# Sparse attention and MoE in one kernel: query chunks shifted by one block, units dealt to steps by time

## The chip, the core and the metric

One core of a Trainium2 chip runs one launch. The time is the device time of that launch in microseconds; what is compared is the median of several runs. TensorE (PE) does matmuls and transposes, VectorE (DVE) and ScalarE (ACT) the elementwise work, GpSimd (POOL) copies and issues transfers, SyncE (SP) only issues transfers. Sixteen DMA engines carry what all of them issue.

## The reference

Block-sparse attention over four batches, eight heads, 768 positions in 24 blocks of 32, head size 64. Each query block sees its neighbours, the first and the last block, and three sampled blocks; the first and the last query block see everything. The result, as 3072 tokens of width 512, goes through a two-layer network.

```python
scores = scale * np.matmul(q, k.transpose(0, 1, 3, 2))
mask = np.abs(blk_i - blk_j) <= window                      # window = 1
mask = mask | (blk_i == 0) | (blk_j == 0) | (blk_i == n_blocks - 1) | (blk_j == n_blocks - 1)
for qb in range(n_blocks):
    for kb in sampled_blocks[qb]:
        mask[qb * block:(qb + 1) * block, kb * block:(kb + 1) * block] = True
scores = np.where(mask, scores, -1000000000.0)
...
out = np.matmul(attn, v)                                    # attn: softmax of scores
...
h = x @ w_in                                                # 512 to 2048
g = h * (1.0 / (1.0 + np.exp(-beta * h)))
return g @ w_out                                            # 2048 to 512
```

## The kernel before

**Chunks and steps.** A batch's 24 query blocks form six chunks of four blocks (128 tokens). A *step* treats one chunk and one half Q of the heads (four heads), so there are 12 steps in a batch and 48 in all. Two chunks of each batch hold a global query block: chunk 0 holds block 0 as its first, chunk 5 holds block 23 as its last. `CHUNK_ORDER` (L48) is 1, 2, 0, 5, 3, 4.

**Keys and values of a chunk.** For each ordinary query block a row of 256 keys is put together in `KG` (`gather_chunk`, L239): 96 neighbours by one copy for the chunk (L248), the first and the last block (L253, only when one of the three buffers is first used in a batch), and three sampled blocks (L259, one copy of 32 columns each, from a register that holds the block's number). Values are gathered from a table in DRAM, `vtab` (`gather_v`, L263): `VA` holds the neighbours and block 0 (L281, L284), `VB` the sampled blocks and the last one. For the blocks of a chunk that are in `direct`, `VB` is fetched by SP, three transfers of 32 rows for each block (L297); for the others by one indirect transfer from GpSimd (L278). Three `VA` and three `VB` buffers go round, and so do three `KG` buffers.

**A step.** `scores` (L303) puts 16 small matmuls into two PSUM banks; VectorE takes the negated maximum (`nm`, L327), ScalarE the exponentials (`probs`, L330). One step later `probs_T` (L337) transposes them on PE, and VectorE copies the result (L345). Another step later `attend` (L384) multiplies by the values: 32 small matmuls for four ordinary blocks (L392), and for a chunk with a global block 24 of these and 24 more over all keys (L404). VectorE divides by the row sum (L410, L411). After both halves of a chunk, `x_transpose` (L427) turns the chunk's output for the network.

**Global query blocks.** `global_scores` (L348) computes both global blocks of two head pairs against all 768 keys: a *global pass*, four in a batch, each with two maxima on VectorE (L364) and two exponentials on ScalarE (L369). `global_T` (L375) transposes it. The layout within a pass is block 0, block 23 for one pair, then for the next. In batch 0 two passes run in step 3 and one each in steps 4 and 5; in later batches one in each of steps 2 to 5 of the batch.

**The network.** Chunks are grouped as `sizes` (L416) says: 2, 2, then five groups of 4. When a group's last chunk is turned, `push_group` (L478) appends 16 first-layer units (`h_unit`, L442: four matmuls, a tanh on ScalarE, a product on VectorE) and the second-layer units of the group before (of the first two groups its own) (`o_unit`, L460: eight matmuls; two units make a chunk's tile, which ScalarE scales and stores, L471 and L473) to one queue, `moe_q`. Each step takes an equal number of units: those in the queue, divided by the steps until the next group is complete (L649 to L654). They are spread over the step around its other work by shares (L721 to L735).

**Order.** The order on PE, GpSimd and SP is that of the program text; each engine works its queue off in order, and a wait holds up all that stands behind it. On GpSimd's queue stand the key gathers, indirect transfers, casts of the next batch (L200, L223) and all loads after the first six: w_in in four pieces (L172), w_out in four (L176), k, q and v of the next batches (L86).

**The opening.** Step 0 starts with half of the heads of two chunks gathered by GpSimd (`kg_half(0, 0)`, `kg_half(1, 0)`, L594 and L595). The other half comes from VectorE in steps 1 and 2 (L667, L674). For the first two chunks one block of four is fetched by SP and three by GpSimd (L600, L601). w_in is issued in step 1 and 2, w_out in steps 5 to 7.

Of the kernel before, what the change touches and what calls it, by code (L numbers as in the profile page):

```python
# [20 lines left out]
def kernel(  # L21
# [26 lines left out]
    CHUNK_ORDER = [1, 2, 0, 5, 3, 4]  # L48
# [106 lines left out]
    def load_regs(t, engine, top, c):  # L155
        i0, i1 = max(4 * c, 1), min(4 * c + 4, NB - 1)
# [82 lines left out]
    def gather_chunk(b, c, KG, p0, p1, eng=None, steady=False):  # L239
        eng = eng or nc.gpsimd  # L240
        js = [j for j in range(4) if 0 < 4 * c + j < NB - 1]
# [3 lines left out]
        for w0 in range(p0, p1, 2):  # L245
            base = kv[:, w0:w0 + 2, (4 * c + j0 - 1) * BLK:(4 * c + j0 + 2) * BLK]
# [10 lines left out]
        for j in js:  # L257
            for r in range(3):
                eng.tensor_copy(  # L259
                    out=KG[:, j, p0:p1, 128 + BLK * r:160 + BLK * r],  # L260
                    in_=kv[:, p0:p1, bass.ds(k_regs[(4 * c + j, r)] * BLK, BLK)])

    def gather_v(b, c, direct=()):  # L263
# [3 lines left out]
        js = [j for j in range(4) if 0 < 4 * c + j < NB - 1]  # L267
# [8 lines left out]
        for j in js:  # L276
            if j not in direct:
                nc.gpsimd.indirect_dma_start(  # L278
                    VB[:, j, :], None, tab[:, :],
                    bass.IndirectOffsetOnAxis(idx_b[:, 4 * c + j:4 * c + j + 1], 0))  # L280
        nc.sync.dma_start(out=VA[0:96, js[0]:js[0] + nj, :],  # L281
                          in_=rows((4 * c + js[0] - 1) * BLK, 96, BLK, nj))
        ga = [j for j in js if 4 * c + j != 1]
        nc.sync.dma_start(out=VA[96:128, ga[0]:ga[0] + len(ga), :],  # L284
                          in_=rows(0, BLK, 0, len(ga)))
        if len(ga) != nj:
            nc.sync.dma_start(out=VA[96:128, 1, :], in_=tab[S:S + BLK, :])
        if direct:
            v_regs = load_regs(sb_eff, ET.SP, NB, c)
            gb = [j for j in direct if 4 * c + j != NB - 2]  # L290
            nc.sync.dma_start(out=VB[96:128, gb[0]:gb[0] + len(gb), :],
                              in_=rows(S - BLK, BLK, 0, len(gb)))
            if len(gb) != len(direct):
                nc.sync.dma_start(out=VB[96:128, NB - 2 - 4 * c, :], in_=tab[S:S + BLK, :])
            for j in direct:
                for r in range(3):
                    nc.sync.dma_start(  # L297
                        out=VB[BLK * r:BLK * (r + 1), j, :],
                        in_=tab[bass.ds(v_regs[(4 * c + j, r)] * BLK, BLK), :])
# [3 lines left out]
    def scores(b, c, Q, KG):  # L303
# [6 lines left out]
        for hp in range(2):  # L310
            for pr in range(2):
                pg = 2 * Q + pr
                for j in range(4):
                    i = 4 * c + j
                    rr = slice(64 * hp, 64 * hp + 64)
                    if 0 < i < NB - 1:
# [31 lines left out]
    def global_scores(b, Q, hp):  # L348
        rr = slice(64 * hp, 64 * hp + 64)
        halves = []  # L350
        for s in range(2):
            sct = ring.tile([P, 512], FP32, tag="bank", name="scg")[:, 0:384]
            halves.append(sct)
            for j in range(4):
                pr, blk = j // 2, (j % 2) * (NB - 1)
# [28 lines left out]
    def attend(b, c, Q, ptT, VA, VB, gTs, x16):  # L384
        av = ring.tile([P, 512], FP32, tag="bank", name="av")[:, 0:4 * VW].rearrange(
            "p (u e) -> p u e", e=VW)
        js = [j for j in range(4) if 0 < 4 * c + j < NB - 1]
# [9 lines left out]
        if len(js) < 4:  # L397
            j = 0 if c == 0 else 3
            bi = 0 if c == 0 else 1
            for u in range(4):  # L400
                pr, hp = u // 2, u % 2
                jj = 2 * pr + bi
                for ct in range(6):
                    nc.tensor.matmul(av[BLK * j:BLK * (j + 1), u, :],  # L404
                                     lhsT=gTs[hp][:, ct, BLK * jj:BLK * (jj + 1)],
                                     rhs=v16[b][:, ct, 4 * Q + u, :],
                                     start=(ct == 0), stop=(ct == 5),
                                     tile_position=(0, BLK * j))
# [51 lines left out]
    def o_unit(gi, s, part):  # L460
# [7 lines left out]
        if part == 1:  # L468
# [3 lines left out]
            r0 = b * S + c * P  # L472
            nc.scalar.dma_start(out=out[r0:r0 + P, :], in_=osb)  # L473
# [28 lines left out]


    steps = []
    for b in range(B):
        for (c, Q) in ((1, 0), (2, 0), (1, 1), (2, 1), (0, 0), (5, 0), (0, 1), (5, 1),
# [273 lines left out]
```

## Time and profile before

| | |
|---|---|
| median of 3 runs | 341.94 us (340.7 to 342.27) |
| the profiled execution | 341.41 us |
| its span, first to last instruction | 339.6 us |
| PE busy | 292.8 us (86%) in 4288 matmuls |
| VectorE busy | 222.4 us (65%) |
| ScalarE busy | 225.7 us (66%) |
| GpSimd busy | 174.3 us (51%) |
| moved by DMA | 56.95 MB |

A profile page gives each engine's busy time, then the span in 40 equal slices (each digit is the busy share of a slice in tenths), the chain of work that ended last, and groups of instructions by source line. Busy time by stretch gives the same for chosen stretches, with PE's granted clock, the mean busy share of the DMA engines (transfers overlap, so it can exceed 1) and GB/s. In a timeline a line has start, length, engine, source line, operation, what it writes from what, and how many are merged. Idle time of an engine that sets nothing costs nothing, and a busy PE need not be at its peak, since matmuls are pipelined.

### The profile page before, as it was taken

The numbers are of one execution on the slowest core, as the hardware profiler recorded it, in microseconds if no ns is written. First come the engines' busy times: TensorE is split into PE (matmuls) and PEld (weight loads), VectorE is DVE, ScalarE is ACT, GpSimd is POOL, SyncE is SP. The second block draws the span as 40 slices with busy tenths as digits, with TensorE's granted clock in tenths as the row PEclk, the third lists the DMA queues.
The fourth block names the chain that finished last, engine by engine and source line by source line (L and its number), as shares of the span: only waits on it lengthen the run. The fifth ranks groups of instructions, "written<-read, shape, count | busy, mean of one in ns | idle before, by whom it ended". The sixth has DMA issues, their size and how long they took to land.

```text
span 339.6 us, 11327 instructions
## 1 busy us (share of the span) xinstructions
PE 292.8 (86%) x4288; PEld 166.1 (49%) x4288; DVE 222.4 (65%) x506; ACT 225.7 (66%) x447; POOL 174.3 (51%) x451
## 2 busy tenths in 40 slices
PE   0554898669787999887999999999989999899995
PEld 0342556545555565544455565454555554444442
DVE  3666878624859777899686668677997576534400
ACT  1693579943768799887688987667776545335411
POOL 5659985629889955879696519725131200000000
PEclk9999999979969999999799999999999999999999
DMA  6979999997698992659898327724162510000021
GB/s 169 377 230 202 292 252 326 274 225 239 169 286 207 314 268 51 173 137 294 183 306 251 75 68 191 178 59 115 35 184 68 135 57 33 31 33 31 32 93 64
DMA packets 40135, 56.95 MB, mean 168 GB/s; under 512 B 7280, under 2 KB 31984, under 8 KB 40080
## 3 DMA queue, kind: packets, MB, share of 16 engines
q0 software_dynamic: 10160, 26.21, 29.2%
q1 hardware_dynamic: 24400, 23.71, 25.7%
q10 hardware_dynamic: 5520, 6.30, 5.4%
q8 instruction: 34, 0.56, 0.7%
q14 instruction: 21, 0.17, 0.2%
HBM read 50.77 MB, written 9.62 MB: 178 GB/s over the span
## 4 chain that ended last, share of the span: by engine, by line
PE 57%; DVE 14%; DMA 10%; ACT 10%; issue 3%; POOL 3%; SPq 1%; another core or an unknown queue 0%; POOLq 0%; DVEq 0%; ACTq 0%
PE ops L465 21%; PE hps L448 19%; PE tp_p L341 5%; ACT probs L330 5%; DVE nm L327 4%; DVE g L454 4%; DMA w_out_sb<-in_moe_w_out_dram 4%; DMA st_kq<-in_k_dram 4%; PE sc L320 3%; PE av L392 3%; DMA st_q<-in_q_dram 3%; ACT t_sb L452 2%; PE av L404 2%; DVE gnm L364 2%; PE tp_x L434 1%
## 5 line engine op out<-in xcount | busy, mean ns | idle before, releaser
L448 PE MATMUL hps<-xT,w_in_sb 128*128 128x512 f16 (+1 forms) x448 | 99.2, 360 | 1.9 <-DVE gnm L366 0.7
L454 DVE SCALAR_TENSOR_TENSOR g<-t_sb,hps 128x512 f16<-128x512 f16 (+1 forms) x112 | 66.8, 609 | 46.9 <-ACT t_sb L452 44.2
L465 PE MATMUL ops<-w_out_sb,g 128*128 128x512 f16 x384 | 89.6, 379 | 3.8 <-DMA w_out_sb<-in_moe_w_out_dram 3.8
L452 ACT ACTIVATE t_sb<-hps,beta_h_sb 128x512 f16<-128x512 f32 (+1 forms) x112 | 70.3, 647 | 29.4 <-PE hps L448 26.4
L330 ACT ACTIVATE probs<-sc,nm 128x256 f16<-128x256 f32 x192 | 76.9, 485 | 18.2 <-DVE nm L327 14.3
L327 DVE TENSOR_REDUCE nm<-sc 128x2 f32<-128x512 f32 x96 | 62.9, 684 | 20.0 <-PE sc L320 16.5
L278 POOL DMA_INDIRECT VB<-vtab,idx_b x40 | 38.9, 972 | 71.5 <-PE av L392 55.9
L259 POOL COPY KG<-kT 128x128 f16 (+1 forms) x264 | 62.8, 293 | 3.0 <-PE sc L320 1.9
L448 PEld LDWEIGHTS <-w_in_sb 128*128 128x128 f16 x448 | 42.8, 101 | 35.3 <-issue 5.2
L465 PEld LDWEIGHTS <-g 128*128 128x128 f16 x384 | 36.8, 98 | 45.8 <-issue 4.7
L248 ACT COPY KG<-kT 128x768 f16<-128x768 f16 (+1 forms) x44 | 34.6, 793 | 11.3 <-PE sc L320 7.1
L345 DVE COPY probsT<-tp_p 128x1024 f16<-128x1024 f16 x48 | 32.3, 673 | 4.8 <-PE hps L448 1.7
L341 PE MATMUL tp_p<-identity,probs 128*128 128x128 f16 x384 | 32.2, 231 | 1.2 <-ACT probs L330 0.6
L471 ACT ACTIVATE osb<-ops 128x512 f32<-128x512 f32 x24 | 14.4, 601 | 28.0 <-PE ops L465 27.9
L320 PE MATMUL sc<-KG,qT 64*32 64x256 f16 x704 | 25.0, 294 | 7.5 <-DVE KG L259 5.1
L341 PEld LDWEIGHTS <-probs 128*128 128x128 f16 x384 | 23.9, 103 | 5.2 <-issue 2.0
L392 PEld LDWEIGHTS <-probsT 128*32 128x32 f16 x1408 | 17.4, 100 | 18.1 <-issue 14.1
L369 ACT ACTIVATE gp<-scg,gnm 128x384 f16<-128x384 f32 x32 | 16.9, 581 | 13.7 <-DVE gnm L366 7.5
L392 PE MATMUL av<-VA,probsT 128*32 128x65 f16 x704 | 22.1, 203 | 2.8 <-issue 2.7
L392 PE MATMUL av<-VB,probsT 128*32 128x65 f16 x704 | 21.8, 201 | 2.9 <-DMA VB<-vtab 2.2
L411 DVE TENSOR_TENSOR x<-av,rec 128x256 f16<-128x256 f32 x48 | 20.1, 420 | 0.8
L207 PE MATMUL tp_k<-identity,k 128*128 128x128 f16 x96 | 9.1, 242 | 12.3 <-ACT k L200 12.1
(69 smaller groups left out, 280.1 us busy)
## 6 DMA issues: line engine op xcount, KB each, us to landing
VA<-vtab SPq DMA_DIRECT2D x16, 390.0 KB
out_dram<-osb ACTq DMA_DIRECT2D x24, 256.0 KB
VB<-vtab SPq DMA_DIRECT2D x147, 32.5 KB
st_k<-in_k_dram POOLq DMA_DIRECT2D x6, 768.0 KB
st_q<-in_q_dram POOLq DMA_DIRECT2D x6, 768.0 KB, 9.3
st_v<-in_v_dram POOLq DMA_DIRECT2D x6, 768.0 KB, 9.7
VA<-vtab SPq DMA_DIRECT2D x8, 292.5 KB
vtab<-v POOLq DMA_DIRECT2D x3, 780.0 KB
```

The costliest lines, as they stand in the source:

```text
L248: (nc.scalar.copy if steady else nc.vector.tensor_copy)(out=KG[:, j0:j1, w0:w0 + 2, 0:96], in_=dataclasses.replace(base, ap=[ap[0], [BLK, ...
L259: eng.tensor_copy(out=KG[:, j, p0:p1, 128 + BLK * r:160 + BLK * r], in_=kv[:, p0:p1, bass.ds(k_regs[(4 * c + j, r)] * BLK, BLK)])
L278: nc.gpsimd.indirect_dma_start(VB[:, j, :], None, tab[:, :], bass.IndirectOffsetOnAxis(idx_b[:, 4 * c + j:4 * c + j + 1], 0))
L320: nc.tensor.matmul(scs[hp][BLK * j:BLK * (j + 1), pr, :], lhsT=qT[b][rr, pg, i * BLK:(i + 1) * BLK], rhs=rhs, start=True, stop=True, tile_ ...
L327: nc.vector.tensor_reduce(out=nm[:, hp, :], in_=scs[hp], axis=AX.X, op=ALU.max, negate=True)
L330: last_exp[0] = nc.scalar.activation(out=pt[:, 2 * pr + hp, :], in_=scs[hp][:, pr, :], func=AF.Exp, bias=nm[:, hp, pr:pr + 1], scale=1.0)
L341: nc.tensor.transpose(out=tp[:, u * 256 + half * P:u * 256 + (half + 1) * P], in_=pt[:, u, half * P:(half + 1) * P], identity=identity)
L392: nc.tensor.matmul(av[BLK * j:BLK * (j + 1), u, :], lhsT=ptT[:, u, half, BLK * j:BLK * (j + 1)], rhs=V[:, j, h * VW:(h + 1) * VW], start=( ...
L448: nc.tensor.matmul(hp[:, 0:n], lhsT=w_in_sb[:, cc, f * P:(f + 1) * P], rhs=xT_tiles[gi][:, cc, 0:n], start=(cc == 0), stop=(cc == N_DMC - 1))
L452: nc.scalar.activation(out=t_sb[:, 0:n], in_=hp[:, 0:n], func=AF.Tanh, bias=0.0, scale=beta_h_sb[:, f:f + 1])
L454: nc.vector.scalar_tensor_tensor(out=g_tiles[gi][:, f, 0:n], in0=t_sb[:, 0:n], scalar=1.0, in1=hp[:, 0:n], op0=ALU.add, op1=ALU.mult)
L465: nc.tensor.matmul(op, lhsT=g_tiles[gi][:, f, s * P:(s + 1) * P], rhs=w_out_sb[:, f, :], start=(f == 0), stop=(f == N_FFC - 1))
```

## The change

**Chunks.** Chunk c now holds blocks 4c - 1 to 4c + 2, so chunk 0 holds blocks 23, 0, 1 and 2, and the others have four ordinary blocks. The order is 1, 2, 3, 4, 5, 0, in pairs of chunks. A chunk's rows in the output are contiguous except chunk 0's, which are stored in two transfers.

**Global rows.** The pass now lays out block 23 before block 0, so that both global rows of a pair stand side by side. `attend` computes them together for chunk 0: 24 matmuls with 64 columns of weights instead of twice 24 with 32. In batch 0 the passes run in steps 4, 5, 10 and 11, in later batches in steps 1 to 4 of the batch.

**The opening.** The second halves of the first two key gathers go from VectorE to GpSimd; the first w_in piece is issued before the values of the first two chunks, of which SP now fetches all four blocks. Of the third and fourth chunk SP fetches three blocks, in chunk 0 of batch 0 both, in chunk 0 of later batches one; elsewhere two. The transposes of batch 1's k and q move one step later.

**Dealing.** A unit has a cost in PE columns: 4096 for a second-layer unit, for a first-layer unit four times the tokens of its group (at least 320). A step's budget is the cost of all units in the queue, divided by one step more than there are until the next group; units are run until a target is met, and what a step overruns or leaves over is carried to the next.

```diff
-    CHUNK_ORDER = [1, 2, 0, 5, 3, 4]
+    CHUNK_ORDER = [1, 2, 3, 4, 5, 0]
...
-        js = [j for j in range(4) if 0 < 4 * c + j < NB - 1]
+        js = [2, 3] if c == 0 else [0, 1, 2, 3]
...
-                    i = 4 * c + j
+                    i = (4 * c + j - 1) % NB
...
-                pr, blk = j // 2, (j % 2) * (NB - 1)
+                pr, blk = j // 2, (NB - 1, 0)[j % 2]
...
-        if len(js) < 4:
-            j = 0 if c == 0 else 3
-            bi = 0 if c == 0 else 1
+        if c == 0:
             for u in range(4):
                 pr, hp = u // 2, u % 2
-                jj = 2 * pr + bi
                 for ct in range(6):
-                    nc.tensor.matmul(av[BLK * j:BLK * (j + 1), u, :],
-                                     lhsT=gTs[hp][:, ct, BLK * jj:BLK * (jj + 1)],
+                    nc.tensor.matmul(av[0:2 * BLK, u, :],
+                                     lhsT=gTs[hp][:, ct, 2 * BLK * pr:2 * BLK * (pr + 1)],
                                      rhs=v16[b][:, ct, 4 * Q + u, :],
                                      start=(ct == 0), stop=(ct == 5),
-                                     tile_position=(0, BLK * j))
+                                     tile_position=(0, 0))
...
-            nc.scalar.dma_start(out=out[r0:r0 + P, :], in_=osb)
+            if c > 0:
+                nc.scalar.dma_start(out=out[r0:r0 + P, :], in_=osb)
+            else:
+                nc.scalar.dma_start(out=out[b * S:b * S + 96, :], in_=osb[BLK:P, :])
+                nc.scalar.dma_start(out=out[(b + 1) * S - BLK:(b + 1) * S, :],
+                                    in_=osb[0:BLK, :])
...
+    def moe_cost(f, a):
+
+        return 8 * D_MODEL if f is o_unit else N_DMC * max(320, P * len(groups[a[0]]))
+
+    moe_done = [0.0]
+
+    def run_moe_to(target):
+
+        while moe_q:
+            cost = moe_cost(*moe_q[0])
+            if moe_done[0] + 0.5 * cost > target:
+                break
+            run_moe(1)
+            moe_done[0] += cost
...
-        for (c, Q) in ((1, 0), (2, 0), (1, 1), (2, 1), (0, 0), (5, 0), (0, 1), (5, 1),
-                       (3, 0), (3, 1), (4, 0), (4, 1)):
+        for (c, Q) in ((1, 0), (2, 0), (1, 1), (2, 1), (3, 0), (4, 0), (3, 1), (4, 1),
+                       (5, 0), (5, 1), (0, 0), (0, 1)):
...
-                trs[5 + a] += [tr("kkqq"[a], a % 2, 0), tr("kkqq"[a], a % 2, 1)]
+                trs[6 + a] += [tr("kkqq"[a], a % 2, 0), tr("kkqq"[a], a % 2, 1)]
...
-                direct = {0: (1, 2, 3), 5: (0, 1, 2)}
+                direct = {0: (2, 3), 3: (0, 1, 2), 4: (0, 1, 2)}
             else:
-                direct = {0: (1, 2), 5: (0, 1)}
+                direct = {0: (2,)}
...
-    prefetch_v(0, (3,))
-    prefetch_v(1, (3,))
+    load_w_in(0)
+    prefetch_v(0, (0, 1, 2, 3))
+    prefetch_v(1, (0, 1, 2, 3))
...
+        pt = scores(b, c, Q, KGs[(b, c)])
+        pend_T.append((b, c, Q, pt))
+        if n == 4:
+            do_X()
         if next_group < len(groups):
             need = sum(sizes[:next_group + 1])
-            gap = max(1, 2 * need + 2 - n)
+            gap = max(1, 2 * need + 2 - n) + 1
         else:
             gap = max(1, len(steps) - n)
-        units = -(-len(moe_q) // gap)
+        target0 = moe_done[0] + moe_carry
+        budget = max(0.0, sum(moe_cost(*u) for u in moe_q) - moe_carry) / gap
...
-            kg_half(0, 1, nc.vector)
-            load_w_in(0)
+            kg_half(0, 1)
+        elif n == 2:
+            do_T()
+            kg_half(1, 1)
             load_w_in(1)
             load_quad("k", k, 1, 0, None, nc.gpsimd)
             load_quad("k", k, 1, 1, None, nc.gpsimd)
-        elif n == 2:
-            do_T()
-            kg_half(1, 1, nc.vector)
             load_w_in(2)
             load_w_in(3)
...
             do_T()
-            do_G(0, 0)
             do_A()
             pend_A.rotate(-1)
             do_A()
             do_T()
-            do_GT()
+            do_X()
             do_A()
-            do_G(0, 1)
             do_A()
-            do_X()
-            do_GT()
             st_v1.append(big("st_v1"))
-            run_moe(2)
...
-        if n > SPB and 2 <= sidx <= 5:
-            acts.append((0.55, lambda: do_G(b, sidx - 2)))
-        elif n in (4, 5):
-            acts.append((0.55, lambda: do_G(b, n - 2)))
+        g_steps = (4, 5, 10, 11) if b == 0 else (1, 2, 3, 4)
+        if sidx in g_steps:
+            acts.append((0.45, lambda: do_G(b, g_steps.index(sidx))))
         if pend_X:
-            acts.append((0.85, do_X))
-        done = 0
+            acts.append((1.0, do_X))
         for share, f in sorted(acts, key=lambda a: a[0]):
-            upto = int(units * share + 0.5)
-            run_moe(upto - done)
-            done = upto
+            run_moe_to(target0 + share * budget)
             f()
-        run_moe(units - done)
+        run_moe_to(target0 + budget)
+        moe_carry = target0 + budget - moe_done[0] if moe_q else 0.0
```

## The prediction

> **What bounds the kernel now.** I read the page's slices first, then busy time by stretch (each stretch ends where a pass of the main loop, a "step", issues its first score matmul, or where a transfer lands), then the chain of waits, then the queues of GpSimd and SP in the opening.
>
> ```profile
> PE   0554898669787999887999999999989999899995
> PEclk9999999979969999999799999999999999999999
> DMA  6979999997698992659898327724162510000021
> ```
>
> Three regimes: until about 80 us PE is half idle while the DMA row stands at 9; until about 160 us everything is busy and nothing is full; from there PE is full.
>
> ```profile
> core 0: us, PE busy (x) PEld busy (x) DVE busy (x) ACT busy (x) POOL busy (x), PEclk, DMA share, GB/s
> 19.40:28.00 8.60, 6.33 (x68) 4.01 (x69) 6.42 (x30) 5.85 (x11) 4.81 (x5) 1.00 0.66 184
> 28.00:77.20 49.20, 36.03 (x627) 24.41 (x627) 31.85 (x78) 35.20 (x75) 34.73 (x82) 0.97 1.12 263
> ...
> 81.84:160.04 78.20, 67.05 (x1342) 42.51 (x1341) 64.13 (x143) 64.55 (x136) 63.80 (x164) 0.96 0.75 215
> 160.04:279.06 119.02, 117.34 (x1778) 63.64 (x1776) 88.83 (x184) 87.48 (x171) 55.27 (x147) 0.99 0.51 138
> 279.06:339.60 60.54, 55.77 (x410) 25.99 (x408) 20.88 (x37) 22.35 (x36) 0.00 (x0) 0.99 0.12 44
> ```
>
> 81.84 is the start of step 10, 160.04 of step 27, 279.06 of step 47, the last. From 28 to 77.2 the DMA engines are full (share 1.12; before that 0.66). From step 10 to 27 PE idles 78.20 - 67.05 = 11.15 us while VectorE, ScalarE and GpSimd are each busy 82%. From step 27 PE idles 1.68 us in 119.
>
> ```profile
> 44.74 1.66 POOL k L200 x4
> 46.68 9.63 DMA st_q<-in_q_dram
> ...
> 63.67 0.69 POOL w_out_sb L176
> 64.36 12.81 DMA w_out_sb<-in_moe_w_out_dram
> 77.21 4.48 PE ops L465 x20
> ```
>
> The chain in the opening runs through GpSimd's queue into transfers: the last piece of w_out is issued at 63.7, lands at 77.2, and only then do the second-layer matmuls of step 9 run. Work that PE does before 77.2 is hidden under these transfers; work after it counts.
>
> **The parts, each with its cost.** The sum is made against the profiled execution, 341.41 us with a span of 339.6; it lies 0.5 us under the median of 341.94. Start-to-start rates on PE from the full stretch: scores of a step 0.36, an attend without global rows 0.36 and with them 0.98, transposed probabilities 0.46, a chunk's x transposes 0.3, four first-layer matmuls 0.86 (0.44 at 256 columns), eight second-layer matmuls 1.73, one global pass 0.44 for scores and 0.34 for transposes.
>
> *Global rows.* 16 attends with them become 8, now 64 columns wide: 8 x (0.98 - 0.36) = 5.0 us of PE less. The trace has no 64-column weight load at this matmul. If it cost nothing extra and the 16 ordinary matmuls beside it shrank in proportion, such an attend takes 0.80; if load and matmul ran one behind the other at the 55 ns of a 128-column transpose, 24 x 0.055 + 0.36 = 1.68. The row it is nearest to is the 32-column one (29 ns each), so I take 0.90; the ends are -0.8 and +6.2 us over eight attends, the latter unlikely.
>
> *What is moved out of the hidden opening.* Three of batch 0's four such attends ran before step 10; now its two run in steps 13 and 14. Two of batch 0's four global passes go from step 3 to 10 and 11, and eight second-layer matmuls from step 9 to 11. I counted the PE instructions of both orders by step at these rates. Step 10 to 26: 59.8 before, 62.1 after. Step 27 to 46: 112.6 and 103.7. Step 47 to the end: 55.1 and 61.4 (the reserve leaves 96 first-layer and 168 second-layer matmuls there; it was 88 and 152). From step 10 on that is 227.5 against 227.2: the saving of the global rows is nearly all given back, because half of what is saved or moved had cost nothing.
>
> *Opening.* On SP, V rows of the first two chunks go from 6 block copies to 24, of the third stays 9 and of the fourth 9. On GpSimd six indirect gathers (21.9 to 29.2, 7.3 us) go and the second halves of two key gathers come from VectorE: 2 x (0.74 + 2.17) = 5.8 us by the rows here.
>
> ```profile
> 12.73 2.99 POOL L259 COPY KG<-kT 128x64 f16 x12
> ...
> 16.36 2.17 POOL L259 COPY KG<-kT 128x64 f16 x12
> ```
>
> VectorE's scattered gather held back step 3's scores until 32.4; that wait goes, and the next thing late there is the second chunk's V. The first w_in piece is issued at 18.5 instead of 29.2, into the stretch with spare DMA: (1.12 - 0.66) x 8.6 / 1.12 = 3.5 us of full-rate transfer, the most by which the last w_out piece could land earlier. Against it: GpSimd's next indirect gathers now wait for the second chunk's attend (I put it near 47, it was 40.2), so its key casts and the loads behind them start some 5 us later. The load issued at 46.68 took 9.63 us, so there is a backlog that covers most of this. I take 77.2 as unchanged, with -3.5 and +6 as ends. After it step 9 has 12 second-layer matmuls left instead of 20: -8 x 0.216 = **-1.7**.
>
> The Trainium skill, Advanced Engine Details and Errata, section Mode Summary, says that GpSimd instructions and VectorE's two-port modes block each other at a shared port. The 2.99 us row ran beside VectorE's casts, the 2.17 us row mostly not, which agrees. By that rule the moved gathers would cost 2 x (0.74 + 2.99) = 7.5 us, the w_in and k loads behind them start 1.7 later, and the sum would be at most 1.7 higher.
>
> *Steps 10 to 26.* PE has 2.3 us more work but 11.15 us of idle to put it in. VectorE gets three more global passes at 1.5 (0.93 + 0.07 + 0.5) and one first-layer unit less, +3.8 on 64.1. At the present 82% that makes 67.9/0.82 = 82.8, +4.6. But in the last five of these steps it runs at 94%:
>
> ```profile
> 139.33:160.04 20.71, 16.37 (x350) 9.46 (x349) 19.41 (x40) 16.70 (x35) 18.38 (x50) 1.00 0.77 209
> ```
>
> At 94% throughout: 67.9/0.94 = 72.2, -6. What speaks for a higher share: units are dealt by time, so PE work per step spreads over 1.9 to 5.4 us instead of 1.9 to 6.4, and GpSimd no longer waits 9.1 us (65.1 to 74.2) for a V buffer, so batch 1's table and gathers come some 8 us earlier, out of the crush at 92 to 96 us where all engines paused. I take the middle, **0**. Batch 1's k and q transposes one step later, and x transposes at the end of a step, I cost at nothing: q is needed at step 12 and ready after step 9, and units held back fill PE behind the x transposes; without that cover each of the 9 in this stage would show its 0.4 us copy.
>
> *Steps 27 to 46.* 112.6 became 119.0, an overhead of 6.4. 103.7 + 6.4 = 110.1; in steps 31 and 32 ScalarE needs about 5.3 us (1.56 for four probs, 0.6 for KG, 1.2 for two t_sb, 1.6 for two qT, 0.3 for half an osb), as much as PE, for which I add 1: 111.1, **-7.9**. VectorE, now 88.8 of 119, would be at 80%.
>
> *Tail.* 61.4 - 55.1 = +6.3, and the last tile is now the one stored in two parts, one more issue on ScalarE's queue (0.34): **+6.6**. PE is alone there, so this is added in full.
>
> Sum: -1.7 + 0 - 7.9 + 6.6 = -3.0, so 341.4 - 3.0 = **338.4 us**.
>
> **Rivals.** Half a per cent (1.7 us) is about what a measurement can tell from no change: faster is under 340.2, slower over 343.7.
>
> *SP becomes the bound of the opening (slower).* Place: the second chunk's attend in step 3. Blocks cost 0.52 to 1.09 us each:
>
> ```profile
> 23.89 2.25 SPq L297 DMA_DIRECT2D VB<-vtab  x3
> ...
> 29.76 1.57 SPq L297 DMA_DIRECT2D VB<-vtab  x3
> ...
> 35.47 9.80 SPq L297 DMA_DIRECT2D VB<-vtab  x9
> ```
>
> From 20.98 with two headers (2.9 and 3.6): 24 x 0.52 ends at 40.0, 24 x 0.75 at 45.5, 24 x 1.09 at 53.6. I forecast with the middle one. At the last, GpSimd (its own rows added up bring it there at about 44) is held some 10 us; less the backlog of about 4, the last w_out piece lands 6 later: 338.4 + 6 = **344.4**. It decides once that attend starts after about 50. For: the DMA engines would be full from about 19. Against: the 1.09 row had six loads queued with it, here it is one until 28, when about half of the blocks are out.
>
> *VectorE stays at 82% in steps 10 to 26* and takes the deferred global passes at full price: 338.4 + 4.6 = **343.0**, no change that can be measured. For: the 82% holds over 78 us of quite different steps. The dealing then does not do what it says: it moves 6.3 us of PE work into the tail without shortening what was in front.
>
> *The middle closes up:* -5 in steps 10 to 26 (nearly 94%; no pause at 92 us, no half clock from 93 to 100): **333.4**. For: PE's pauses there follow the late opening. Against: the mix still needs three engines in turn in each step.
>
> **Chances.** Forecast 0.43 (its own range 336 to 340.2), SP 0.20, VectorE 0.20, the middle closing 0.17. So faster 0.43 + 0.17 = 0.60, same 0.20, slower 0.20. The range reaches to the SP case and short of the best: 332.5 to 344.5. It leaves out a 64-column load at its worst.
>
> **What would show it.** Right: the last w_out piece lands within 2 us of 77; step 10 starts at 79 to 82; steps 10 to 26 take 76 to 80 us, 27 to 46 about 111, the rest about 67; a global attend takes 0.8 to 1.0. Wrong: the second chunk's attend after 50 (SP); steps 10 to 26 over 81 (VectorE) or under 75; PE idle between steps 27 and 46, which would mean that the work held back for the tail was missed there.

## The result, and the profile after

| | median us | ratio to the kernel before (95%) |
|---|---|---|
| before | 342.11 (340.7 to 342.75, 4 runs) | |
| changed | 363.07 (361.39 to 363.46, 4 runs) | 1.0609 (1.0562 to 1.0656) |

The forecast was 338.4 us and faster; the changed kernel is 6.1% slower and outside the range. The ratios of this document leave out executions more than 1.5% above the shortest one of the same kernel. The profiled execution has a span of 361.2 us, 21.6 more than before. The first two views are the slices of the page and the busy time by stretch; the stretches begin at the same steps as those of the prediction (10, 27, 47).

```profile
PE   0563337868998967988899599899999999999995
...
PEclk9999999887999896999999699999999999999999
DMA  6998978998679868338976723565136411010021
```

```profile
core 0: us, PE busy (x) PEld busy (x) DVE busy (x) ACT busy (x) POOL busy (x), PEclk, DMA share, GB/s
91.36:177.15 85.79, 73.27 (x1341) 45.15 (x1340) 66.60 (x152) 67.75 (x141) 62.92 (x155) 0.94 0.72 195
177.15:293.86 116.71, 110.43 (x1633) 59.46 (x1631) 86.08 (x180) 83.55 (x167) 54.94 (x144) 0.97 0.51 134
293.86:361.20 67.34, 62.51 (x450) 29.99 (x448) 22.88 (x41) 24.85 (x40) 0.00 (x0) 1.00 0.12 44
```

Step 10 starts 9.5 us later than before, steps 10 to 26 take 7.6 more, steps 27 to 46 only 2.3 less, the tail 6.8 more. The tail is what was forecast. The rest is not, and it has a mark that the busy columns do not explain: VectorE, ScalarE and GpSimd are busy for 63 to 68 of 85.79 us, so none of them is full, and PE idles 12.5 us there and 6.3 in the stretch in which it had idled 1.7. Something holds up queues that the busy columns do not count.

The chain of waits says where. The first line is the page's sum by engine, the others are a stretch of the chain (start, us, what):

```profile
PE 50%; POOL 10%; DMA 10%; issue 10%; ACT 7%; DVE 7%; SPq 4%; POOLq 2%; ACTq 0%
...
117.98 0.55 POOLq L158
118.53 4.81 issue
123.50 0.12 POOL KG L260
...
128.43 0.78 POOLq L158
129.21 2.01 issue
131.39 0.12 POOL KG L260
```

"issue" (time in which an engine waits for nothing that the profile shows) was 3% of the chain and is 10%. On GpSimd it stands ahead of the key gathers, behind line 158. That line is `load_regs`, which loads a chunk's block numbers from an SBUF table into registers, and register instructions are not counted as busy. Its own rows, asked for by source line (queue, operation, count, duration in ns as least/median/most, first and last start), before:

```profile
L157 POOLq TENSOR_LOAD <-sb_raw x24: 806/820/2098, 5.5 to 251.1; - x24
L157 SPq TENSOR_LOAD <-sb_eff x24: 744/758/1901, 21.9 to 267.9; - x24
L157 DVEq TENSOR_LOAD <-sb_raw x2: 859/971/1083, 22.6 to 25.9; - x2
```

and in the changed kernel:

```profile
L158 POOLq TENSOR_LOAD <-sb_raw x26: 1385/2721/5608, 5.4 to 271.7; - x26
L158 SPq TENSOR_LOAD <-sb_eff x24: 1265/2474/3334, 21.7 to 286.1; - x24
```

The two loads on VectorE's queue belong to the key gathers that the change moves to GpSimd; either kernel has 50 loads in all. The median is 3.3 times as long. All of GpSimd's loads added up go from 25.6 to 74.0 us, SP's from 24.2 to 56.9. The diff touches this function in one line, which the cut diff above leaves out:

```diff
-        i0, i1 = max(4 * c, 1), min(4 * c + 4, NB - 1)
+        i0, i1 = max(4 * c - 1, 1), 4 * c + 3
...
             t[0:1, 3 * i0:3 * i1], engines=[engine], min_val=0, max_val=top,
```

A block has three numbers of four bytes. Before, the numbers of a chunk start at byte 48c, now at 48c - 12. 48c is a multiple of 16, 48c - 12 never is.

What one such load does is seen in step 18 (130.94 to 139.80; it took 3.2 before). GpSimd's timeline (start, us, engine, line, operation, in brackets the idle time before it) and the PE row that ends the pause:

```profile
123.47 2.89 POOL L260 COPY KG<-kT 128x128 f16 x12 [4.94 <-issue]
...
131.35 2.89 POOL L260 COPY KG<-kT 128x128 f16 x12 [2.14 <-PE sc L321]
134.39 1.02 POOL L279 DMA_INDIRECT VB<-vtab,idx_b  x1
135.72 1.00 POOL L279 DMA_INDIRECT VB<-vtab,idx_b  x1 [0.31 <-issue]
136.71 1.85 POOL L201 CAST k<-st_k 128x384 f16<-128x384 f32 x4
```

```profile
137.74 1.71 PE L208 MATMUL tp_k<-identity,k 128*128 128x128 f16 x12 [5.46 <-POOL k L201]
```

The load at 117.7 took 5.61 us, the one at 128.4 took 2.73. Behind them stand the key gathers, behind the second of those two indirect gathers of values and then a cast of the next batch's keys, and PE's transposes of these keys are written into step 18 in program order: PE waits 5.46 us with other work behind it. Of the 4.94 us ahead of the first gathers the view names no releaser, only "issue"; the load from 117.7 to 123.3 covers them. The granted clock of this step is 0.81, and over steps 10 to 26 it is 0.94.

### The profile page after: what moved, and what is told of

The parts are those of the page before. It is cut to its first block, busy times and chain, and to the rows that moved or that the text cites. A ratio compares the mean times of both kernels' runs of the same rounds, so it can differ in the third digit from the quotient of the medians.

```text
span 361.2 us, 10938 instructions
## 1 busy us (share of the span) xinstructions
PE 296.1 (82%) x4096; PEld 165.7 (46%) x4096; DVE 217.8 (60%) x478; ACT 225.5 (62%) x447; POOL 177.8 (49%) x476
## 4 chain that ended last, share of the span: by engine, by line
PE 50%; POOL 10%; DMA 10%; issue 10%; ACT 7%; DVE 7%; SPq 4%; POOLq 2%; ACTq 0%
PE ops L464 20%; PE hps L447 16%; PE tp_p L342 4%; DMA VB<-vtab 4%; DMA st_kq<-in_k_dram 3%; PE av L393 3%; DMA w_out_sb<-in_moe_w_out_dram 3%; POOL KG L260 3%; ACT probs L331 3%; PE sc L321 2%; SPq L298 2%; POOL v L224 2%; POOL VB L279 2%; POOL k L201 2%; DVE nm L328 2%
## 5 line engine op out<-in xcount | busy, mean ns | idle before, releaser
L464 PE MATMUL ops<-w_out_sb,g 128*128 128x512 f16 x384 | 93.5, 391 | 3.8 <-DMA w_out_sb<-in_moe_w_out_dram 3.7
L451 ACT ACTIVATE t_sb<-hps,beta_h_sb 128x512 f16<-128x512 f32 (+1 forms) x112 | 68.9, 645 | 32.6 <-PE hps L447 29.2
L260 POOL COPY KG<-kT 128x128 f16 (+1 forms) x288 | 67.6, 288 | 18.3 <-issue 14.4
L328 DVE TENSOR_REDUCE nm<-sc 128x2 f32<-128x512 f32 x96 | 62.1, 684 | 20.6 <-PE sc L321 19.6
L279 POOL DMA_INDIRECT VB<-vtab,idx_b x37 | 36.0, 973 | 57.1 <-PE av L393 43.4
L249 ACT COPY KG<-kT 128x768 f16<-128x768 f16 (+1 forms) x44 | 34.3, 802 | 29.2 <-PE hps L447 21.6
L393 PEld LDWEIGHTS <-probsT 128*32 128x32 f16 x1408 | 18.2, 99 | 31.7 <-issue 18.1
L208 PE MATMUL tp_k<-identity,k 128*128 128x128 f16 x96 | 10.6, 265 | 20.3 <-ACT k L201 10.5
L254 POOL COPY KG<-kT 128x512 f16<-128x512 f16 (+1 forms) x28 | 15.2, 573 | 18.2 <-ACT kT L212 7.5
```

The lines of the kernel that those rows point to most:

```text
L249: (nc.scalar.copy if steady else nc.vector.tensor_copy)(out=KG[:, j0:j1, w0:w0 + 2, 0:96], in_=dataclasses.replace(base, ap=[ap[0], [BLK, ...
L260: eng.tensor_copy(out=KG[:, j, p0:p1, 128 + BLK * r:160 + BLK * r], in_=kv[:, p0:p1, bass.ds(k_regs[(4 * c + j - 1, r)] * BLK, BLK)])
L279: nc.gpsimd.indirect_dma_start(VB[:, j, :], None, tab[:, :], bass.IndirectOffsetOnAxis(idx_b[:, 4 * c + j - 1:4 * c + j], 0))
L328: nc.vector.tensor_reduce(out=nm[:, hp, :], in_=scs[hp], axis=AX.X, op=ALU.max, negate=True)
L393: nc.tensor.matmul(av[BLK * j:BLK * (j + 1), u, :], lhsT=ptT[:, u, half, BLK * j:BLK * (j + 1)], rhs=V[:, j, h * VW:(h + 1) * VW], start=( ...
L451: nc.scalar.activation(out=t_sb[:, 0:n], in_=hp[:, 0:n], func=AF.Tanh, bias=0.0, scale=beta_h_sb[:, f:f + 1])
```

## The experiments

The kernel before took 340.4 us (median) beside the first four kernels of these experiments (short loads, the two with long loads, the opening's values), 335.9 and 335.8 beside the others. The record names one chip for the 340.4 and the 335.8 and another for the 335.9, so the chip alone doesn't explain the difference; its cause is open. Runs are compared as ratios to the kernel before that ran beside them, and differences of a few tenths of a per cent between such ratios are weak.

**Loads that start on a multiple of 16 bytes.** The tables are shifted by three numbers and a load's start is rounded down to a multiple of four numbers, nothing else.

```diff
-    sb_raw = persist.tile([1, NB * 3], I32, name="sb_raw")
-    nc.vector.tensor_copy(out=sb_raw, in_=sb_i32[0:1, :, 0])
+    PAD = 3
+    sb_raw = persist.tile([1, NB * 3 + 4], I32, name="sb_raw")
+    nc.vector.tensor_copy(out=sb_raw[:, PAD:PAD + NB * 3], in_=sb_i32[0:1, :, 0])
...
+        lo = (PAD + 3 * i0) // 4 * 4
...
-            t[0:1, 3 * i0:3 * i1], engines=[engine], min_val=0, max_val=top,
+            t[0:1, lo:PAD + 3 * i1], engines=[engine], min_val=0, max_val=top,
...
```

(`sb_eff` likewise; the line left out picks the registers from the shifted place.)

> The changed kernel with its two tables of block numbers shifted by three entries, so that the twelve numbers of a chunk start at a multiple of 16 bytes again; nothing else. Theory A (the register loads of the block numbers became slow: on GpSimd 2.7 us instead of 0.82, on SP 2.5 instead of 0.75, because a chunk's numbers now start 12 bytes short of such a multiple): the loads go back to 0.8 and 0.75, the stalls of steps 18 and 30 go, the opening shortens by about 4, and the time falls to 340 to 350 us. Rival B (24 block copies on SP hold the opening back whatever the loads cost): loads may get short, but the second chunk's attend stays after 48 us and the time at 355 or more.

Measured: 344.63 us, ratio 1.0124 (1.0095 to 1.0153). Its load rows and its stretches from steps 10, 27 and 47 (columns as above):

```profile
L161 POOLq TENSOR_LOAD <-sb_raw x26: 562/818/1674, 5.2 to 251.4; - x26
L161 SPq TENSOR_LOAD <-sb_eff x24: 520/752/1582, 21.0 to 265.8; - x24
```

```profile
86.72:164.87 78.15, 69.17 (x1340) 43.23 (x1338) 66.71 (x152) 67.07 (x141) 61.70 (x151) 1.00 0.81 219
164.87:273.54 108.67, 107.33 (x1632) 58.26 (x1630) 86.11 (x180) 82.74 (x167) 54.69 (x144) 1.00 0.52 141
273.54:340.90 67.36, 62.51 (x450) 29.98 (x448) 22.89 (x41) 24.86 (x40) 0.00 (x0) 0.99 0.12 44
```

The starting address of 50 loads is worth 4.9 of the 6.1%. Between the two profiled executions it is 4.6 us in the opening, 7.6 in steps 10 to 26 and 8.0 in steps 27 to 46; the one with short loads is the shortest of its six, so these add up to more than 4.9%. Step 18 falls to 3.0 us. In steps 10 to 26 PE has the matmuls of the changed kernel (1340 and 1341) and is busy 4.1 us less, at a granted clock of 1.00 in place of 0.94, and 73.27 x 0.94 = 68.9 is close to the 69.17 measured: the long loads had cost once as idle time of PE and again as a lower clock.

**The same on the kernel before, the other way round.** The tables of the kernel before are shifted by the same three numbers, with `lo` not rounded, so that every load starts off a multiple of 16.

```diff
+        lo = (PAD + 3 * i0) // 1 * 1
...
-            t[0:1, 3 * i0:3 * i1], engines=[engine], min_val=0, max_val=top,
+            t[0:1, lo:PAD + 3 * i1], engines=[engine], min_val=0, max_val=top,
```

> The kernel before with the same two tables shifted by three entries, so that every chunk's numbers start 12 bytes past a multiple of 16 bytes; nothing else. A: each of the 50 loads takes 2.0 to 2.8 us, and the kernel slows to 348 to 360 us. B: the loads get longer or not, the time stays within 1% of 342.

Measured: 348.75 us, ratio 1.0261 (1.0222 to 1.0299).

```profile
L160 POOLq TENSOR_LOAD <-sb_raw x24: 2044/2718/4413, 5.1 to 255.0; - x24
L160 SPq TENSOR_LOAD <-sb_eff x24: 1864/2472/2957, 21.0 to 271.8; - x24
L160 DVEq TENSOR_LOAD <-sb_raw x2: 2818/2888/2959, 22.3 to 27.5; - x2
```

The loads grow as in the changed kernel and the time follows, though by 2.6% and not 4.9. So the address is the cause with either order of work, and the order of the kernel before makes it about half as dear. In its profiled execution (345.25 us, the shortest of four) steps 10 to 26 take 81.3 us, 3.1 more than before, and 27 to 46 take 118.6, none more; where the rest of the 2.6% lies this trace doesn't show.

**A multiple of 8.** The changed kernel with `PAD = 1` and `lo` not rounded: 48c - 8 bytes.

> The changed kernel with the tables shifted by one entry: a chunk's numbers start at a multiple of 8 bytes that is none of 16. If any multiple of 8 is enough, the loads take 0.8 us and the time is that of the run with multiples of 16. If 16 is needed, they stay at 2.5 to 2.7 us and the time at 360 to 364.

Measured: 359.19 us in one run, 1.055 of the kernel before.

```profile
L161 POOLq TENSOR_LOAD <-sb_raw x26: 782/2722/5189, 5.5 to 268.0; - x26
```

A multiple of 8 does not help. Only chunk 0's loads, whose six numbers start on a multiple of 16 here, are short (the 0.78 of the row). The tables have the same size as in the run with short loads, so it is the start that counts and not the larger tables.

**GpSimd's loads alone.** Only `sb_raw` is shifted, `sb_eff` is not.

```diff
+        pad = PAD if t is sb_raw else 0
+        lo = (pad + 3 * i0) // 4 * 4 if pad else 3 * i0
...
```

> The changed kernel with only GpSimd's table shifted, so that its loads take 0.8 us and SP's still 2.5. If GpSimd's queue carried the cost of the long loads (steps 18 and 30, and the key gathers of the opening): 347 to 351 us, near the run with both short (344.6). If SP's queue carried it (V later by 1.7 us a chunk): 355 us or more.

Measured: 341.38 us, ratio 1.0151 (1.0111 to 1.0192).

```profile
L161 POOLq TENSOR_LOAD <-sb_raw x26: 568/816/1748, 5.2 to 250.8; - x26
L161 SPq TENSOR_LOAD <-sb_eff x24: 1263/2475/3299, 21.1 to 264.7; - x24
```

With SP's loads still three times as long, and on another chip, the interval overlaps that of the run with all loads short. GpSimd's carry most of the loss; of SP's no share is shown, and the intervals leave room for up to 1%.

**Chunk 0's loads in the kernel before.** Eight of its loads (block 1 is the first, byte 12) were long too.

```diff
-        i0, i1 = max(4 * c, 1), min(4 * c + 4, NB - 1)
+        i0, i1 = 4 * c, min(4 * c + 4, NB - 1)
```

> The kernel before, except that chunk 0's block numbers are read from the start of the table (twelve numbers from a multiple of 16 bytes, the first three unused) instead of nine from 12 bytes past it. Its eight loads of 1.9 to 2.1 us fall to 0.8. If they lie on a chain there too, the ratio is 0.985 to 0.995; if they are covered, 0.997 to 1.003.

Measured: 336.49 us, ratio 1.0013 (0.9984 to 1.0042). The eight loads fall from 1.9 to 2.1 us to 0.8, and nothing is gained: one long load in six is covered.

**The opening's values as before.** SP takes one block in four of the first two chunks and GpSimd gathers the others, with the long loads first.

```diff
-    prefetch_v(0, (0, 1, 2, 3))
-    prefetch_v(1, (0, 1, 2, 3))
+    prefetch_v(0, (3,))
+    prefetch_v(1, (3,))
```

> The changed kernel, only that of the first two chunks' V rows one block of four is fetched by SP and three by GpSimd again, as before. A: the two slow loads remain ahead of them, the opening gains 3 to 6 us at most and the later stalls stay: 356 to 360 us. B: step 4 starts near 45 instead of 53 and the time falls to 352 to 355.

Measured: 357.75 us, ratio 1.0501 (1.046 to 1.0542). Step 10 starts at 85.62 instead of 91.36, and step 18 still takes 8.9 us: a second loss of about 1.1%, apart from the loads.

**The same with short loads.** The edit of the first run and this one.

> Short loads (tables shifted by three entries) and the first two chunks' V as before: one block of four from SP, three from GpSimd. Theory V (what is left of the loss is the 24 block copies on SP, which hold the second chunk's attend until 48.5): step 4 starts near 44 instead of 50.6, step 10 near 82 instead of 86.7, and the time falls from 344.6 to 338 to 341. Rival T (the transposes of batch 1's k and q one step later hold GpSimd's q casts, and with them the w_out issues that stand behind): step 4 starts earlier but the last w_out piece still lands after 80 and the time stays at 342 or more.

Measured: 335.86 us, ratio 0.999 (0.9964 to 1.0016), 1.3 points less than with short loads alone (on another chip). What the edit takes away is seen in the run with short loads and all blocks on SP. Its SP and PE timelines:

```profile
22.60 7.74 SPq L301 DMA_DIRECT2D VB<-vtab  x12
...
32.77 11.86 SPq L301 DMA_DIRECT2D VB<-vtab  x12
```

```profile
43.45 0.21 PE L396 MATMUL av<-VB,probsT 128*32 128x65 f16 x1 [1.97 <-DMA VB<-vtab]
...
47.54 0.21 PE L396 MATMUL av<-VB,probsT 128*32 128x65 f16 x1 [2.57 <-DMA VB<-vtab]
48.48 0.22 PE L396 MATMUL av<-VB,probsT 128*32 128x65 f16 x1 [0.72 <-DMA VB<-vtab]
```

SP's last block is issued at 44.6, the second chunk's attend waits block by block until 48.5, and step 4 starts at 50.63. With the values as before it starts at 40.99, and step 10 at 82.70 instead of 86.72.

**Transposes of batch 1 one step earlier**, as before, with short loads, first alone and then with the opening's values as before.

```diff
-                trs[6 + a] += [tr("kkqq"[a], a % 2, 0), tr("kkqq"[a], a % 2, 1)]
+                trs[5 + a] += [tr("kkqq"[a], a % 2, 0), tr("kkqq"[a], a % 2, 1)]
```

> Short loads, V on SP as in the change, but the transposes of batch 1's k and q in steps 5 to 8 as before. V: step 4 stays at 50.6 and the time within 1.5 us of 344.6. T: GpSimd's wait of 8.0 us ahead of the first q cast falls to 4 or less, w_out's last piece lands 3 to 4 earlier, and the time falls to 340 to 342.

Measured: 338.89 us, ratio 1.0109 (1.0068 to 1.015): not to be told from 1.0124. The last w_out piece is issued at 71.27 instead of 75.12 and still lands at 82.95 instead of 83.10.

> Short loads, V and transposes both as before. If V and T hold different stretches of the same chain, this is the fastest: step 10 at 78 to 80 and 335 to 339 us. If one covers the other, it equals the better of the two within 1 us.

Measured: 333.61 us, ratio 0.9961 (0.9926 to 0.9997). Against 0.999 without this edit the intervals overlap, so 0.3% is a lean and not a finding. The traces show what the two edits move together: GpSimd's casts of q, and the w_out issues behind them, in the run with short loads alone

```profile
68.22 1.86 POOL L204 CAST q<-st_q 128x384 f16<-128x384 f32 x4 [8.03 <-PE tp_k L211]
...
74.38 1.49 POOL L180 DMA_DIRECT2D w_out_sb<-in_moe_w_out_dram  x2
```

and in this one:

```profile
61.13 1.86 POOL L204 CAST q<-st_q 128x384 f16<-128x384 f32 x4 [0.71 <-DMA st_q<-in_q_dram]
...
67.73 1.48 POOL L180 DMA_DIRECT2D w_out_sb<-in_moe_w_out_dram  x2
```

The cast needs the buffers that k's transposes on PE set free; it waited 8.03 us for them, and w_out's last pieces stand behind it. Either edit by itself does most of this: the cast starts at 62.89 with the values as before and at 63.26 with the transposes as before, so the transposes add 1.8 us to what the values gain.

**The opening's key gathers as before too** (short loads, values, transposes, and the second halves of the first two key gathers back on VectorE). The order of the w_in and k loads stays as changed; it was not tested.

```diff
-            kg_half(0, 1)
+            kg_half(0, 1, nc.vector)
...
-            kg_half(1, 1)
+            kg_half(1, 1, nc.vector)
```

> Short loads, V and transposes of the opening as before, and now also the second halves of the first two key gathers on VectorE again. If GpSimd's queue is what is late in the opening (its first key cast starts at 52.2 in the run with V and transposes as before, at 44.5 in the kernel before), the cast moves to 45 to 47, w_out's last piece lands 3 to 5 earlier, and the ratio to the kernel before falls from 0.996 to 0.982 to 0.988. If VectorE's scattered gather holds back step 3 as much as GpSimd gains: 0.993 to 1.000.

Measured: 334.14 us, ratio 0.9911 (0.9875 to 0.9947), between the two ranges expected. Its twelve executions spread from 330.85 to 341.5 us, so the ratio rests on seven of them; the median of all twelve is 0.995 of the kernel before. Against 0.9961 the intervals overlap, so no gain over the version with two edits undone is shown. The first key cast does move, from 52.2 to 47.2, and the last w_out issue from 68.5 to 65.0, but in the profiled execution (336.52 us, not one of the seven) step 10 starts only 0.4 us earlier.

**The old dealing** on the version with short loads, values and transposes as before.

```diff
-            gap = max(1, 2 * need + 2 - n) + 1
+            gap = max(1, 2 * need + 2 - n)
...
+        units = -(-len(moe_q) // gap)
...
-            run_moe_to(target0 + share * budget)
+            upto = int(units * share + 0.5)
+            run_moe(upto - done)
```

> As the run with short loads and V and transposes as before, but each step takes an equal number of units again, without the reserve. If the dealing by time is what shortens steps 10 to 46 (forecast: 78 and 111 us, the tail 67): those two stretches together get 6 to 9 longer, the tail 6.5 shorter, and the ratio rises from 0.996 to 1.000 to 1.005. If the dealing only moves work into the tail: the ratio stays within 0.002.

Measured: 336.46 us, ratio 1.0037 (1.0005 to 1.0069), just above the interval of the version with the new dealing (0.9926 to 0.9997), which ran on another chip. Its last two stretches:

```profile
159.46:272.19 112.73, 110.76 (x1652) 59.29 (x1650) 88.16 (x181) 85.08 (x169) 55.28 (x145) 1.00 0.52 140
272.19:334.80 62.61, 57.58 (x426) 27.70 (x424) 20.83 (x37) 22.21 (x36) 0.00 (x0) 1.00 0.12 43
```

The new dealing, with its reserve of one step more, takes 5.6 us out of steps 27 to 46 (107.1 with it) and puts 4.4 into the tail (67.0): 1.2 us net. Step 10 starts at 82.60 instead of 80.75, another 1.9.

**The kernel before again**, to have its stretches on a chip on which it takes as long as beside the version with transposes and values as before.

> The kernel before, unchanged, for its stretches on this chip: step 10 at 80 to 82, 78 us to step 27, 119 to step 47, 60.5 to the end.

Measured: 336.01 us in one run, span 334.2. First this kernel, from steps 10, 27 and 47, then the version with short loads, values and transposes as before:

```profile
82.12:155.41 73.29, 64.41 (x1343) 40.83 (x1341) 63.55 (x143) 63.73 (x136) 63.79 (x163) 1.00 0.84 231
155.41:273.67 118.26, 116.87 (x1778) 63.87 (x1776) 88.53 (x184) 87.53 (x171) 55.38 (x148) 0.99 0.52 138
273.67:334.20 60.53, 55.77 (x410) 25.98 (x408) 20.85 (x37) 22.35 (x36) 0.00 (x0) 0.99 0.12 44
```

```profile
80.75:157.48 76.73, 68.18 (x1340) 42.71 (x1338) 66.90 (x153) 66.81 (x141) 61.09 (x148) 1.00 0.83 226
157.48:264.58 107.10, 106.40 (x1633) 57.74 (x1631) 85.31 (x179) 83.00 (x168) 54.65 (x143) 1.00 0.54 143
264.58:331.60 67.02, 62.51 (x450) 29.97 (x448) 22.87 (x41) 24.85 (x40) 0.00 (x0) 0.99 0.12 44
```

## Why the prediction was wrong

Put together in us by stage; a column is the difference of two profiled executions. The last column is the version with short loads and the opening's values and transposes as before, against the kernel before run again.

| | forecast | changed - before | short loads - before | opening restored - before again |
|---|---|---|---|---|
| to step 10 | -1.7 | +9.5 | +4.9 | -1.4 |
| steps 10 to 26 | 0 | +7.6 | 0.0 | +3.4 |
| steps 27 to 46 | -7.9 | -2.3 | -10.4 | -11.2 |
| tail | +6.6 | +6.8 | +6.8 | +6.5 |
| sum | -3.0 | +21.6 | +1.3 | -2.6 |

**The step that failed: a cost with no term at all.** The prediction's parts treat the shift of the chunks as a change of PE work alone ("Global rows", "What is moved out of the hidden opening"), and GpSimd's time as "its own rows added up". The register loads are no such row: the page counts them nowhere as busy. That their address moves by 12 bytes was in the diff, and that some loads of the kernel before took 1.9 to 2.1 us instead of 0.8 was in its trace, under the source line of `load_regs`. In the changed kernel long loads are 4.9 of the 6.1%, and the cause is shown from both sides: by taking them away from the changed kernel, and by putting them into the one before.

**"SP becomes the bound of the opening" happened, at the place and near the price named, and the threshold was wrong.** With short loads the second chunk's attend has its last values at 48.5, 1.5 us after the 47 of the forecast and before the 50 from which it was to decide. Yet w_out's last piece lands at 83.1 (issued at 75.12, 7.98 us on the way) instead of 77.2: the rival's 6. The term that was mis-sized is the queue's delay: "its key casts and the loads behind them start some 5 us later". The first key cast starts 7.5 later (52.0, before 44.5) and the last w_out issue 10.7 later (75.1, before 64.4).

The way of the last piece is 4.8 us shorter than before (7.98 against 12.81), close to the 4 of backlog that were taken. Yet the issue alone does not set the landing: with the transposes one step earlier it comes 3.9 us sooner and the piece lands at 82.95 all the same. What is missing then is transfer: from 44 to 52, while GpSimd waits 7.1 us for these values, the DMA share is 0.81, where it was 1.19 in the kernel before. This fits a late landing; no run tests it alone. In the changed kernel the attend waits until 51.3, past the threshold, because loads of 2.67 and 2.47 us, in place of 0.96 and 0.75, stand ahead of the two chunks' blocks on SP, and w_out lands at 87.7. What the rival had wrong is the path: with the values back on GpSimd the first key cast is no earlier (52.4), but PE reaches step 4 9.6 us earlier and with it k's transposes.

**"Batch 1's k and q transposes one step later ... I cost at nothing" looked at q's user and not at GpSimd's queue.** The cover named (q is needed at step 12) is there, but the casts of q wait for these transposes, and the w_out issues wait behind the casts. The price is small and unclear, 0.3% between overlapping intervals, and none can be told while the values on SP hold PE anyway (1.0109 against 1.0124).

**Key gathers on GpSimd, 5.8 us.** The moved gathers took 1.05 + 2.17 + 0.74 + 2.17 = 6.1 us in the changed kernel. By the shared port of the Trainium skill (Advanced Engine Details and Errata, section Mode Summary) the estimate had been 7.5; none of the 2.17 us rows was slowed, so this place does not bear on it. As places in the queue they put off the first key cast by 5.0 us (52.2 against 47.2); what that costs in time is not shown.

**Steps 10 to 26, 0.** Once loads and opening are out of the way these steps take 3.4 us more than before: PE's busy time grows by 3.8 and its idle time stays (8.9 and 8.6 us). The hope that the additional work would go into the idle time failed, and the rival "VectorE stays at 82%" gave the better size, +4.6. VectorE is 86.7% busy before and 87.2% after. ScalarE and PE also keep their shares, so it isn't shown that VectorE sets it. The 78.2 us of the first trace contained a pause with a stretch at half clock (0.51 from 93 to 100 us, the 6 in its PEclk row) that the second trace of the same kernel, 73.29 us at 1.00, doesn't have: the base itself was 5 us off.

**Steps 27 to 46, -7.9,** came out at -10.4 to -11.2. The overhead of 6.4 was carried over whole and 1 was added for ScalarE. Of the 11.2, PE's busy time is 10.5 (116.87 to 106.40, where the count had 8.9) and its idle time 0.7 (1.4 to 0.7). So the overhead was mostly busy time above the count, and it shrank (from 4.3 to 2.7) where the forecast kept it. **The tail, +6.6,** was right within 0.2.

That the last column's sum of -2.6 lies near the forecast -3.0 is luck: +3.4 in steps 10 to 26 and -3.3 against the forecast in steps 27 to 46 cancel.

**A global attend at 0.90.** It takes 1.23 from start to start. The rows of its matmul and of its weight load, changed kernel:

```profile
L403 PEld LDWEIGHTS <-gpT x192: 106/112/114, 104.3 to 312.5; 128*64 128x64 f16 x192
L403 PE MATMUL av<-v,gpT x192: 192/196/218, 104.3 to 312.5; 128*64 128x65 f16 x192
```

The weight load takes 112 ns instead of 96 with 32 columns, the matmul as long as before. The 24 wide matmuls start 31 ns apart, where the 32-column ones started 29 apart, so the row that the forecast took as nearest was right and this is only 0.05 of the difference. The rest lies where the two kinds meet: before, the first global matmul started 0.15 us into the attend, among the ordinary ones and some 0.01 after the start of the one ahead; now it starts at 0.35, 0.12 after the last ordinary one. No run separates the reasons. Eight of them save 16 x 0.98 - 8 x (1.23 + 0.36) = 3.0 us of PE, not the 5.0 of the forecast (5.6 at 0.90), and still inside the ends that were given.

**What the change is worth without its two accidents.** In ratios: 6.1% as made; 1.2 with the loads' address mended; -0.1 with the opening's values as before and -0.4 with the transposes as well. With the key gathers too it is -0.9 by the seven executions of the ratio and -0.5 by the median of all twelve. So what is left is a gain of some 0.4 to 0.9%, of the 0.9 that was forecast for the whole (3.0 of 341.4 us), and the lower end is close to no change (interval to 0.9997). The dealing is some 0.8 points of it (0.9961 against 1.0037, two chips); the shift and the paired global rows by themselves have no run.

Left open: why some loads take 4 to 5.6 us, beyond what their address explains; why the kernel before covers half of its long loads and the changed one less; which of the opening's two small edits is worth what. Mending the changed kernel's address by starting the loads one block earlier instead of shifting the table wasn't tried.

## What to carry to other kernels

A shift of indices moves addresses, also those of small loads into registers: look in the diff for every table that is read at a new offset, and ask the trace for its source line, since busy columns do not hold such instructions. When every engine has idle time and the chain fills up with "issue", ask what the in-order queue does there that isn't counted. A transfer or cast at the end of a queue is moved by every wait ahead of it, so a "hidden" edit has to be followed through the queues of its user's user, here transposes, casts, w_out.

## What the hardware showed

**Register loads go by fours.** Loads of four-byte numbers from SBUF: off a multiple of 16 bytes 12 numbers take 2.72 us on GpSimd and 2.47 on SP, nine 2.05 and 1.87, six 1.39 and 1.27: some 0.23 and 0.21 for each number. On a multiple of 16, 12 take 0.82 and 0.75, eight 0.56 and 0.52, six 0.80 and 0.73: some 0.25 to 0.28 for each full group of four and as much for each single number left over (worked out from these durations; no instruction is seen below the load). A start on a multiple of 8 is as slow as one on 4. The Trainium skill, DMA: Bandwidth & Descriptors, section Latency and other measured facts, gives such a load a floor of about 600 ns; the shortest here took 520, so in this case it lies lower.

**A block fetch on SP has no fixed price.** The same transfers of 32 rows took 0.65 us each (7.74 for 12) and right after it 0.99 (11.86 for 12) in the run with short loads. What slows them wasn't tested.
